# DMA transposes, and a first batch pipelined by head pairs, in a fused attention and MLP kernel

## The chip, the cores and the metric

The kernel runs on one core of one Trainium2 chip. The metric is the device time of the whole program in microseconds (us), as the median over several executions; lower is better.

## The reference, cut to what matters

There are 8 batches, 12 heads, 448 positions and a head size of 64, so the model width is 768.

```python
q_n, k_n = rmsnorm(q, g_q), rmsnorm(k, g_k)        # over the 64 of a head, gains per channel
attn = softmax(q_n @ k_n.T / 8)                    # 448 x 448 for each head
x = concat_heads(attn @ v)                         # batch x 448 x 768
u = x + ((x.T @ U) @ V).T                          # mixing along the sequence, rank 32
out = u + relu(u @ w_ch1) @ w_ch2                  # 768 -> 3072 -> 768
```

## The kernel before

Positions lie on partitions (112 at a time). A "pair" `p` is two heads; a "tile" `t` is four heads, so two pairs; a batch has six pairs and three tiles. q and k are normalised in that layout and must then be turned so that the head channel lies on partitions. The MLP needs u turned in the same way. Both are done on TensorE:

```python
def transposes(p):                                  # eight 112x128 blocks through TensorE
    pt = ps_o.tile([P, 2, S], BF16, tag="o")
    for s in range(2):
        for j in range(NJ):
            nc.tensor.transpose(pt[:, s, j * SP:(j + 1) * SP], qkn[...], ident[:SP, :SP])
    nc.vector.tensor_scalar(qT, pt[:, 0], gg, None, OP.mult)     # both gains, on the way out of PSUM
    nc.vector.tensor_copy(kT, pt[:, 1])

def mix_u(b, dc):                                   # u turned: low-rank part + x times identity
    nc.tensor.matmul(pu, t4s[b][:, ds], V4, start=True, stop=False)
    for i, off in enumerate(OFFS[par]):
        nc.tensor.matmul(pu[:, lo:hi], xt[i][:, ds], ident[:, ...], start=False, stop=(i == 3))
    ...                                             # copies to uA, uB

# in mlp(b): the low-rank product again, for the residual in the output layout
nc.tensor.matmul(po, V4[:, off:off + P], t4s[b][:, hs], start=True, stop=False)
for hc in range(KH):
    nc.tensor.matmul(po, hT[:, hc, i * P:(i + 1) * P], w2b[:, hc, hs], start=False, ...)
```

The program first does the attention and the mixing of batch 0 (the "head"), and then, for each batch, weaves the attention of the next batch between the MLP products of this one. Every engine runs its own instructions in program order; the first hole below shows it (ACT stood still for 10.34 us before one instruction, while the exponential behind it had its scores ready).

```python
for _, piece in attention(0, head=True): piece()
for _, piece in mixing(0): piece()
for b in range(B):
    fill, total = mlp(b), volume(b % 2)
    weave(fill, total * 0.86, attention(b + 1))     # attention spread over 86% of the MLP
    weave(fill, total * 0.11, mixing(b + 1))
```

## Time and profile before

The time is 657.54 us (657.22 to 657.66, 3 executions). PE is TensorE, PEld the loading of its weights, DVE is VectorE, ACT is ScalarE, POOL is GpSimd, SP is the engine that issues most DMAs.

| | before |
|---|---|
| profiled span | 655.2 us |
| first MLP product (end of the head) | 67.3 us |
| PE busy from there to the end | 582 of 588 us |
| PE busy in the head from 20 to 60 us | 52% to 62% |

This is the table of stretches of the kernel before; it gives the busy us of each engine in each stretch, in the order PE, PEld, DVE, ACT, POOL, with the number of instructions, then the granted TensorE clock, the mean busy share of the DMA engines, and GB/s.

```profile
20.00:30.00 10.00, 6.01 (x56) 3.53 (x56) 7.59 (x13) 4.63 (x7) 6.73 (x5) 0.50 0.77 122
30.00:40.00 10.00, 6.22 (x69) 3.83 (x68) 6.06 (x18) 4.36 (x5) 1.66 (x1) 0.67 1.18 253
40.00:50.00 10.00, 5.16 (x56) 3.42 (x57) 5.60 (x14) 3.73 (x6) 10.00 (x9) 0.50 1.06 213
67.20:655.00 587.80, 582.33 (x4834) 332.05 (x4834) 303.60 (x682) 202.51 (x302) 89.60 (x57) 1.00 0.28 70
```

In the head PE is half idle and its clock is cut to 0.50 to 0.67. From the first MLP product on, PE is full at full clock. DMA is over-full (above 1) from 30 us on, because the weights come in; it stays so until about 90 us.

This is the chain of waits of the kernel before, inside one MLP: start, length, what. (The chain is followed back from the last instruction, at each step to what released it.)

```profile
236.42 1.08 PE ph L286 x6
237.50 0.39 PE pt L190 x8
237.89 1.95 PE ph L286 x12
```

```profile
281.13 0.19 PE pu L263
281.32 0.20 PE pu L266 x4
281.51 0.97 PE po L306 x6
```

The chain is nothing but PE here, one group behind the other, so its lengths are prices: eight transposes cost 0.39 to 0.40 us, one mixing group 0.39 us, six output products 0.97 us (0.162 each).

### The profile page before, as it was taken

The numbers are of one execution on the slowest core, as the hardware profiler recorded it, in microseconds if no ns is written. First come the engines' busy times: TensorE is split into PE (matmuls) and PEld (weight loads), VectorE is DVE, ScalarE is ACT, GpSimd is POOL, SyncE is SP. The second block draws the span as 40 slices with busy tenths as digits, with TensorE's granted clock in tenths as the row PEclk, the third lists the DMA queues.
The fourth block names the chain that finished last, engine by engine and source line by source line (L and its number), as shares of the span: only waits on it lengthen the run. The fifth ranks groups of instructions, "written<-read, shape, count | busy, mean of one in ns | idle before, by whom it ended". The sixth has DMA issues, their size and how long they took to land.

```text
span 655.2 us, 12039 instructions
## 1 busy us (share of the span) xinstructions
PE 623.4 (95%) x5198; PEld 355.5 (54%) x5198; DVE 346.3 (53%) x773; ACT 231.0 (35%) x341; POOL 120.8 (18%) x98
## 2 busy tenths in 40 slices
PE   6556999999999999999999999999999999999997
PEld 2334565654556555654456556654556656554464
DVE  4757766555544575565644666655544465252211
ACT  5443453244431444224522254315432164402100
POOL 2465132202202022202202022202020200000000
PEclk9566999999999999999999999999999999999999
DMA  7999983421305213503305033413314100010011
GB/s 171 171 234 225 226 184 89 110 72 38 86 25 133 70 41 85 133 26 85 86 25 131 27 86 86 109 49 85 78 32 105 54 2 2 25 49 1 0 50 48
DMA packets 47445, 54.59 MB, mean 83 GB/s; under 512 B 3744, under 2 KB 43808, under 8 KB 47392
## 3 DMA queue, kind: packets, MB, share of 16 engines
q1 hardware_dynamic: 39200, 44.39, 26.8%
q0 software_dynamic: 7872, 9.44, 8.4%
q8 instruction: 40, 0.66, 0.4%
q14 instruction: 13, 0.11, 0.1%
q10 hardware_dynamic: 320, 0.00, 0.0%
HBM read 52.25 MB, written 11.01 MB: 97 GB/s over the span
## 4 chain that ended last, share of the span: by engine, by line
PE 89%; DVE 3%; ACT 2%; DMA 1%; POOL 1%; issue 0%; POOLq 0%
PE po L306 34%; PE ph L286 33%; PE o L225 8%; PE sc L204 7%; PE pt L190 3%; PE pu L263 2%; PE pu L266 2%; ACT E_95 L209 1%; DMA qk<-in_q_dram 1%; PE po L304 1%; DVE rstd L165 1%; DVE qkn L179 1%; ACT hT L289 1%; PE pm L250 1%; POOL sq L160 1%
## 5 line engine op out<-in xcount | busy, mean ns | idle before, releaser
L306 PE MATMUL po<-w2b,hT 128*128 128x384 bf16 x1344 | 244.5, 326 | 0.0
L306 PEld LDWEIGHTS <-hT 128*128 128x128 bf16 x1344 | 124.5, 98 | 82.6 <-issue 10.3
L286 PEld LDWEIGHTS <-w1b 128*128 128x128 bf16 x1152 | 104.5, 98 | 98.8 <-issue 14.2
L160 POOL TENSOR_TENSOR sq<-qk 112x1024 f32<-112x1024 f32 x44 | 83.2, 1907 | 381.9 <-DVE rstd L165 188.8
L289 ACT ACTIVATE hT<-ph 128x384 bf16<-128x384 f32 (+1 forms) x96 | 52.1, 543 | 234.1 <-PE ph L286 234.1
L286 PE MATMUL ph<-uB,w1b 128*128 128x512 bf16 x576 | 133.0, 379 | 0.0
L209 ACT ACTIVATE E_96<-sc 112x896 bf16<-112x896 f32 x96 | 86.2, 911 | 80.4 <-PE sc L204 80.3
L209 ACT ACTIVATE E_95<-sc 112x896 bf16<-112x896 f32 x96 | 85.4, 912 | 60.2 <-PE sc L204 60.2
L286 PE MATMUL ph<-uA,w1b 128*128 128x384 bf16 x576 | 105.3, 326 | 0.1
L291 DVE TENSOR_SCALAR hT<-ph 128x384 bf16<-128x384 f32 (+1 forms) x96 | 59.8, 623 | 83.9 <-PE ph L286 83.5
L179 DVE TENSOR_TENSOR qkn<-qk,rstd 112x512 bf16<-112x512 f32 x96 | 66.6, 734 | 1.8 <-ACT rstd L171 1.4
L204 PE MATMUL sc<-qT,kT 64*112 64x448 bf16 x384 | 63.2, 394 | 2.9 <-ACT E_95 L209 1.2
L165 DVE TENSOR_REDUCE rstd<-sq 112x16 f32<-112x1024 f32 x48 | 56.3, 1210 | 10.1 <-ACT sq L158 6.6
L228 DVE RECIPROCAL rec<-o 128x4 f32<-128x4 f32 x96 | 17.3, 180 | 62.0 <-PE o L225 61.6
L194 DVE TENSOR_SCALAR qT<-pt,gg 128x448 bf16<-128x448 bf16 x48 | 21.5, 448 | 46.7 <-PE pt L190 46.6
L225 PEld LDWEIGHTS <-E_95 112*128 112x128 bf16 x768 | 32.1, 101 | 20.1 <-DVE xs_100 L232 8.6
L204 PEld LDWEIGHTS <-kT 64*112 64x112 bf16 x384 | 20.7, 130 | 37.7 <-issue 34.2
L225 PEld LDWEIGHTS <-E_96 112*128 112x128 bf16 x768 | 32.3, 102 | 12.2 <-DVE xs_100 L232 3.9
L190 PE MATMUL pt<-ident,qkn 112*128 112x112 bf16 x384 | 28.5, 218 | 5.9 <-DVE qkn L179 4.8
L190 PEld LDWEIGHTS <-qkn 112*128 112x128 bf16 x384 | 23.9, 100 | 16.3 <-DVE qkn L179 7.1
L272 DVE CAST uB<-pu 128x448 bf16<-128x448 f32 x24 | 14.5, 620 | 8.6 <-PE pu L266 8.6
L195 DVE COPY kT<-pt 128x448 bf16<-128x448 bf16 x48 | 18.3, 381 | 0.0
(102 smaller groups left out, 354.7 us busy)
## 6 DMA issues: line engine op xcount, KB each, us to landing
qk<-in_q_dram SPq DMA_DIRECT2D x24, 448.0 KB, 4.4
qk<-in_k_dram SPq DMA_DIRECT2D x24, 448.0 KB, 5.9
vt<-in_v_dram SPq DMA_DIRECT2D x24, 448.0 KB, 6.8
w1b<-in_moe_w_ch_dram POOLq DMA_DIRECT2D x6, 768.0 KB, 12.3
w2b<-in_moe_w_ch_dram POOLq DMA_DIRECT2D x6, 768.0 KB, 28.4
out_dram<-osb SPq DMA_DIRECT2D x8, 336.0 KB, 2.8
out_dram<-osb SPq DMA_DIRECT2D x8, 288.0 KB, 2.7
out_dram<-osb SPq DMA_DIRECT2D x8, 240.0 KB, 2.6
```

Source lines behind the costliest of these rows:

```text
L160: nc.gpsimd.tensor_tensor(sqs[t, s], qks[t][:, s], qks[t][:, s], OP.mult)
L165: nc.vector.tensor_reduce(rstds[t][:, s].rearrange("p h j -> p (h j)"), sqs.pop((t, s)).rearrange("p h (j d) -> p (h j) d", d=D), AX, OP.add)
L179: nc.vector.tensor_tensor(qkns[t][:, pr, s].rearrange("p j h d -> p h j d"), qk[:, s, hp].rearrange("p h (j d) -> p h j d", d=D), rstd[:, ...
L190: nc.tensor.transpose(pt[:, s, j * SP:(j + 1) * SP], qkn[:, p % 2, s, j].rearrange("p h d -> p (h d)"), ident[:SP, :SP])
L194: nc.vector.tensor_scalar(qT, pt[:, 0], gg, None, OP.mult)
L204: nc.tensor.matmul(sc[:, hh, 0:S], kT[pp, kc * SP:(kc + 1) * SP], qT[pp, :], start=True, stop=True)
L209: nc.scalar.activation(Es[p % NE][:, :, PAD + kc * S:PAD + (kc + 1) * S], scs.pop((p, kc))[:, :, 0:S], AF.Exp, scale=float(D) ** 0.5)
L225: nc.tensor.matmul(o[:, i, :], E[:, hh, c:c + P], va[:, hl, kc, :], start=(kc == 0), stop=(kc == NJ - 1))
L286: nc.tensor.matmul(ph, w1b[:, dc, hc * P:(hc + 1) * P], u[:, dc, :], start=(dc == 0), stop=(dc == KD - 1))
L289: nc.scalar.activation(hT[:, hc, 0:n], ph, AF.Relu)
L291: nc.vector.tensor_relu(hT[:, hc, 0:n], ph)
L306: nc.tensor.matmul(po, hT[:, hc, i * P:(i + 1) * P], w2b[:, hc, hs], start=False, stop=(hc == KH - 1))
```

## The change

The intent is to take work off the full TensorE, and to shorten the head:

- The transposes of q and k become one DMA transpose per pair, except for the first 8 pairs. The gains are then a separate VectorE step.
- The mixing adds the low-rank part to x in place, in the output layout; u is turned by DMA. The output stage no longer repeats the low-rank product.
- Batch 0 is a pipeline by head pairs: its mixing is done per pair on TensorE, the first load is split in halves, pair 6 (of batch 1) runs in the head too, and filler products are to hold the clock up.
- The squares of tile 2 move from POOL to ACT, and are computed in pair 0. The attention of the next batch is pressed into 77% of the MLP (86% before), so that 14% stay for the DMA transposes of u to land.

```diff
-    NE, NV, NWARM, NFILL = 2, 3, 30, 0
+    NE, NV, NWARM, NH = 2, 3, 16, 3
+    FA, FM, NPE = 0.77, 0.09, 8
@@ squares
-            if t < 2:
+            if t < 3:
                 nc.scalar.activation(...Square)
@@ transposes
+        if p < NPE:
+            ...                                   # on TensorE, as before
+        else:
+            nc.sync.dma_start_transpose(qkT.rearrange("d s (j p) -> d (s j) p", j=NJ), qkn)
+    def gains(p):
+        if p >= NPE:
+            nc.vector.tensor_scalar(qkTs[p][:, 0], qkTs[p][:, 0], gg, None, OP.mult)
@@ mixing
+    def mix_u(b, i):                              # for two halves of 384 columns
+            nc.tensor.matmul(pu, lhsT, t4s[b][:, hs], start=True, stop=True)
+            nc.vector.tensor_add(xt[rows, hs], pu[rows, :], xt[rows, hs])
+    def mix_uT(b, i):
+            nc.sync.dma_start_transpose(us[b][:, :, i * P:(i + 1) * P], ...)
@@ mlp
-                    nc.tensor.matmul(po, V4[:, off:off + P], t4s[b][:, hs], start=True, stop=False)
@@ attention, one pair (cut): scores, expo, transposes(p+1), ..., values(p-1, 0)
+            add(0, scale, t + 1, odd)
             add(1, scores, p, (2, 3))
             ...
             add(1, values, p - 1, 1)
             ...
+                add(0, gains, p + 1)              # last VectorE step before the next pair's scores
             ...
             add(0, load, t + 3)                   # every second pair
@@ head (cut)
+        load(0, 2); load(1); load_v(0); ...
+        squares(1); scale(0, 1)
+        load_mix()                                # 14 small DMAs of U, one of V
+        load(2); load_v(1); load_v(2)
+        cast_v(0); load_w1(0); load_w1(1)
+        for p in range(7):
+            scores(p, (0, 1)); expo(p, 0)
+            if p > 1: mix_a(0, p - 2)
+            transposes(p + 1)
+            ...                                   # heat(NH): three filler products, twice a pair
+            squares(t + 2, ss=(odd,))             # at p = 0 this is tile 2, on ACT
+            expo(p, 3)
+            ...
@@ schedule
+        head()
+        for i in range(6): load_w2(i)
+                rest = [mix_u(0, i) for i in range(4)] + attention(1, 1)
```

More of the change, by code (lines that the diff above doesn't have):

```diff
@@ L113, in load_mix @@
                     nc.sync.dma_start(Uf[r:r + p1 - p0, par, i, :], Ur[j, p0:p1, :])
-        for i in range(4):
-            nc.sync.dma_start(Vf[i * rank:(i + 1) * rank, :], moe_V)
+        nc.sync.dma_start(Vf, moe_V.rearrange("r s -> () r s").to_broadcast([4, rank, S]))
     def setup_mix():
@@ L135, with load @@
     NT, NP = B * 3, B * 6
-    qks, vts, sqs, rstds, qkns, qTs, scs, x3_of = {}, {}, {}, {}, {}, {}, {}, {}
-    def load(t):
-        b, h0 = t // 3, (t % 3) * HG
-        qk = loads.tile([SP, 2, HG, NJ * D], FP32, tag="qk")
-        nc.sync.dma_start(qk[:, 0], q[b, h0:h0 + HG].rearrange("h (p j) d -> p h (j d)", j=NJ))
-        nc.sync.dma_start(qk[:, 1], k[b, h0:h0 + HG].rearrange("h (p j) d -> p h (j d)", j=NJ))
-        qks[t] = qk
+    qks, vts, sqs, rstds, qkns, qkTs, scs, x3_of = {}, {}, {}, {}, {}, {}, {}, {}
+    def load(t, parts=1):
+        b, h0, n = t // 3, (t % 3) * HG, HG // parts
+        qks[t] = loads.tile([SP, 2, HG, NJ * D], FP32, tag="qk", name="qk")
+        for h in range(0, HG, n):
+            for s, src in enumerate((q, k)):
+                nc.sync.dma_start(qks[t][:, s, h:h + n],
+                                  src[b, h0 + h:h0 + h + n].rearrange("h (p j) d -> p h (j d)", j=NJ))
     def load_v(t):
@@ L152, in cast_v, with squares, reduce, rsqrt @@
         nc.gpsimd.tensor_copy(vas[t % NV][:, :, :, 0:D], vts.pop(t).rearrange("p h (j d) -> p h j d", d=D))
-    def squares(t):
-        for s in range(2):
-            sqs[t, s] = norm.tile([SP, HG, NJ * D], FP32, tag="sq", name="sq")
-            if t < 2:
-                nc.scalar.activation(sqs[t, s], qks[t][:, s], AF.Square)
-            else:
-                nc.gpsimd.tensor_tensor(sqs[t, s], qks[t][:, s], qks[t][:, s], OP.mult)
-    def reduce(t):
-        rstds[t] = norm.tile([SP, 2, HG, NJ], FP32, tag="rstd", name="rstd", bufs=3)
-        for s in range(2):
-            nc.vector.tensor_reduce(rstds[t][:, s].rearrange("p h j -> p (h j)"),
-                                    sqs.pop((t, s)).rearrange("p h (j d) -> p (h j) d", d=D), AX, OP.add)
-    def rsqrt(t):
-        rs = rstds[t].rearrange("p s h j -> p (s h j)")
+    ALL = slice(0, HG)
+    def squares(t, hs=ALL, ss=(0, 1)):
+        for s in ss:
+            if (t, s) not in sqs:
+                sqs[t, s] = norm.tile([SP, HG, NJ * D], FP32, tag="sq", name="sq")
+            if t < 3:
+                nc.scalar.activation(sqs[t, s][:, hs], qks[t][:, s, hs], AF.Square)
+            else:
+                nc.gpsimd.tensor_tensor(sqs[t, s][:, hs], qks[t][:, s, hs], qks[t][:, s, hs], OP.mult)
+    def reduce(t, hs=ALL, ss=(0, 1)):
+        if t not in rstds:
+            rstds[t] = norm.tile([SP, 2, HG, NJ], FP32, tag="rstd", name="rstd", bufs=3)
+        for s in ss:
+            nc.vector.tensor_reduce(rstds[t][:, s, hs].rearrange("p h j -> p (h j)"),
+                                    sqs[t, s][:, hs].rearrange("p h (j d) -> p (h j) d", d=D), AX, OP.add)
+    def rsqrt(t, hs=ALL):
+        rs = rstds[t][:, :, hs].rearrange("p s h j -> p s (h j)")
         nc.scalar.activation(rs, rs, AF.Ln, bias=eps)
@@ L185, in transposes @@
     def transposes(p):
-        qkn = qkns[p // 2]
-        pt = ps_o.tile([P, 2, S], BF16, tag="o")
-        for s in range(2):
-            for j in range(NJ):
-                nc.tensor.transpose(pt[:, s, j * SP:(j + 1) * SP],
-                                    qkn[:, p % 2, s, j].rearrange("p h d -> p (h d)"), ident[:SP, :SP])
-        qT = attn.tile([P, S], BF16, tag="qT")
-        kT = attn.tile([P, S], BF16, tag="kT")
-        nc.vector.tensor_scalar(qT, pt[:, 0], gg, None, OP.mult)
-        nc.vector.tensor_copy(kT, pt[:, 1])
-        qTs[p] = qT, kT
+        qkn = qkns[p // 2][:, p % 2].rearrange("p s j h d -> p (s j) (h d)")
+        qkT = attn.tile([P, 2, S], BF16, tag="qkT")
+        qkTs[p] = qkT
+        if p < NPE:
+            pt = ps_mm.tile([P, 2, S], BF16, tag="mm")
+            for i in range(2 * NJ):
+                nc.tensor.transpose(pt.rearrange("d s (j p) -> d (s j) p", j=NJ)[:, i, :], qkn[:, i, :], ident[:SP, :SP])
+            nc.vector.tensor_scalar(qkT[:, 0], pt[:, 0], gg, None, OP.mult)
+            nc.vector.tensor_copy(qkT[:, 1], pt[:, 1])
+        else:
[3 more added lines that the diff above has]
+            nc.vector.tensor_scalar(qkTs[p][:, 0], qkTs[p][:, 0], gg, None, OP.mult)
     def scores(p, kcs):
-        qT, kT = qTs[p]
+        qT, kT = qkTs[p][:, 0], qkTs[p][:, 1]
         for kc in kcs:
@@ L220, in values @@
         d0 = (2 * (p % 6) + hh) * D
-        o = ps_o.tile([P, 4, D + 1], FP32, tag="o")
+        if p < 6 and hh:
+            o = ps_mm.tile([P, 4, D + 1], FP32, tag="mm")
+        else:
+            o = ps_o.tile([P, 4, D + 1], FP32, tag="o")
         for i, off in enumerate(OFFS[par]):
@@ L253, in mix_t @@
         t4s[b] = t4b
-    def mix_u(b, dc):
-        par = b % 2
-        if dc == 0 and par == 0:
-            us["A"] = upool.tile([P, KD, 384], BF16, tag="uA", name="uA")
-            us["B"] = upool.tile([P, KD, 512], BF16, tag="uB", name="uB")
-        uA, uB, xt = us["A"], us["B"], x_tiles(b)
-        ds = slice(dc * P, (dc + 1) * P)
-        pu = ps_mm.tile([P, S], FP32, tag="mm")
-        nc.tensor.matmul(pu, t4s[b][:, ds], V4, start=True, stop=False)
-        for i, off in enumerate(OFFS[par]):
-            lo, hi = max(off, 0), min(off + P, S)
-            nc.tensor.matmul(pu[:, lo:hi], xt[i][:, ds], ident[:, lo - off:hi - off],
-                             start=False, stop=(i == 3))
-        if par == 0:
-            nc.vector.tensor_copy(uA[:, dc, :], pu[:, 0:384])
-            nc.vector.tensor_copy(uB[:, dc, 0:64], pu[:, 384:448])
-        else:
-            nc.vector.tensor_copy(uB[:, dc, 64:512], pu)
+    def mix_u(b, i):
+        par, off = b % 2, OFFS[b % 2][i]
+        lhsT = V4[:, off:off + P] if 0 <= off < 384 else Vsh[:, par, :]
+        rows = slice(0, P) if 0 <= off < 384 else slice(64 * par, 64 * par + 64)
+        xt = x_tiles(b)[i]
+        for half in range(2):
+            hs = slice(half * HALF, (half + 1) * HALF)
+            pu = ps_mm.tile([P, HALF], FP32, tag="mm")
+            nc.tensor.matmul(pu, lhsT, t4s[b][:, hs], start=True, stop=True)
+            nc.vector.tensor_add(xt[rows, hs], pu[rows, :], xt[rows, hs])
@@ new lines, in mix_uT, with mix_a @@
+    def mix_uT(b, i):
+        par, off = b % 2, OFFS[b % 2][i]
+        if i == 0:
+            us[b] = upool.tile([P, KD, 384 + 128 * par], BF16, tag=f"u{par}", name=f"u{par}")
+        if par or off < 384:
+            nc.sync.dma_start_transpose(us[b][:, :, i * P:(i + 1) * P],
+                                        x_tiles(b)[i].rearrange("t (c d) -> t c d", d=P))
+    def mix_a(b, dc):
+        xt, cs = x_tiles(b), slice(dc * P, (dc + 1) * P)
+        if dc == 0:
+            us[b] = upool.tile([P, KD, 384], BF16, tag="u0", name="u0")
+            t4s[b] = upool.tile([P, dm], BF16, tag="t4b", bufs=3, name="t4b")
+        pm = ps_mm.tile([P, P], FP32, tag="mm")
+        for i in range(4):
+            nc.tensor.matmul(pm[i * rank:(i + 1) * rank, :], Ub[:, b % 2, i, :], xt[i][:, cs], start=True, stop=True)
+        nc.vector.tensor_copy(t4s[b][:, cs], pm)
@@ L275, in store, with mix_b @@
+    def mix_b(b, dc):
+        xt, cs = x_tiles(b), slice(dc * P, (dc + 1) * P)
+        pu = ps_mm.tile([P, 384], FP32, tag="mm")
+        nc.tensor.matmul(pu, t4s[b][:, cs], V4[:, 0:384], start=True, stop=False)
+        for i in range(3):
+            nc.tensor.matmul(pu[:, i * P:(i + 1) * P], xt[i][:, cs], ident, start=False, stop=(i == 2))
+        nc.vector.tensor_copy(us[b][:, dc, :], pu)
     def store(b, c0, c1, osb, r0):
@@ L281, in mlp @@
         par = b % 2
-        u, n = (us["A"], 384) if par == 0 else (us["B"], 512)
+        u, n = us[b], (384, 512)[par]
         for hc in range(KH):
@@ L299, in mlp @@
                 po = ps_mm.tile([P, HALF], FP32, tag="mm")
-                if off < 0:
-                    nc.tensor.matmul(po, Vsh[:, 0, :], t4s[b - 1][:, hs], start=True, stop=False)
-                    nc.tensor.matmul(po, Vsh[:, 1, :], t4s[b][:, hs], start=False, stop=False)
-                else:
-                    nc.tensor.matmul(po, V4[:, off:off + P], t4s[b][:, hs], start=True, stop=False)
                 for hc in range(KH):
                     nc.tensor.matmul(po, hT[:, hc, i * P:(i + 1) * P], w2b[:, hc, hs],
-                                     start=False, stop=(hc == KH - 1))
+                                     start=(hc == 0), stop=(hc == KH - 1))
                     if hc % 6 == 5 and hc != KH - 1:
@@ L317, in mlp, with attention @@
                 yield HALF
-    def attention(b, head=False):
+    def attention(b, start=0):
         items = []
@@ L324, in add @@
             items.append((weight, lambda: fn(*args)))
-        for p in range(b * 6, b * 6 + 6):
+        for p in range(b * 6 + start, b * 6 + 6):
             t, odd = divmod(p, 2)
-            late = head and p == 0
             add(1, scores, p, (0, 1))
             add(0, expo, p, 0)
-            if head and p == 1:
-                add(0, scale, 1, 0)
             if p + 1 < NP:
                 add(1, transposes, p + 1)
-            if odd and t + 2 < NT:
-                add(0, reduce, t + 2)
-            if late:
-                add(0, reduce, 1)
             add(1, expo, p, 1)
+            if not odd and t + 1 < NT:
+                add(0, rsqrt, t + 1)
             if p % 6:
                 add(1, values, p - 1, 0)
-            if not odd:
-                if t + 1 < NT and not late:
-                    add(0, scale, t + 1, 0)
-                if t + 2 < NT:
-                    add(0, squares, t + 2)
+            if t + 1 < NT:
+                add(0, scale, t + 1, odd)
             add(1, scores, p, (2, 3))
             add(0, expo, p, 2)
-            if odd and t + 2 < NT:
-                add(0, rsqrt, t + 2)
             if p % 6:
                 add(1, values, p - 1, 1)
-            if t + 1 < NT and (p == 1 if head and t == 0 else not odd):
-                add(0, scale, t + 1, 1)
+            if t + 2 < NT:
+                add(0, squares, t + 2, ALL, (odd,))
+            if t + 1 < NT and odd:
                 add(0, cast_v, t + 1)
+            if p + 1 < NP:
+                add(0, gains, p + 1)
+            add(1, expo, p, 3)
+            if t + 2 < NT:
+                add(0, reduce, t + 2, ALL, (odd,))
             if odd and t + 3 < NT:
@@ L358, in attention @@
                 add(0, load_v, t + 3)
-            add(1, expo, p, 3)
-            if late:
-                add(0, rsqrt, 1)
-            if head and p == 2:
-                add(0, setup_mix)
-            if head and p in (0, 2, 3):
-                for i in range((0, 0, 2, 4)[p], (2, 0, 4, 6)[p]):
-                    add(0, load_w1, i)
         add(1, values, b * 6 + 5, 0)
@@ L369, in attention, with head @@
         return items
+    def head():
+        A, Bh = slice(0, 2), slice(2, 4)
+        load(0, 2)
+        load(1)
+        load_v(0)
+        setup()
+        heat(NWARM)
+        squares(0, A)
+        reduce(0, A)
+        squares(0, Bh)
+        rsqrt(0, A)
+        scale(0, 0)
+        nc.vector.tensor_mul(gg, gg, gk2)
+        transposes(0)
+        reduce(0, Bh)
+        rsqrt(0, Bh)
+        squares(1)
+        scale(0, 1)
+        load_mix()
+        load(2)
+        load_v(1)
+        load_v(2)
+        cast_v(0)
+        load_w1(0)
+        load_w1(1)
+        for p in range(7):
+            t, odd = divmod(p, 2)
+            scores(p, (0, 1))
+            expo(p, 0)
+            if p > 1:
+                mix_a(0, p - 2)
+            transposes(p + 1)
+            if p == 0:
+                reduce(1)
+            expo(p, 1)
+            if not odd:
+                rsqrt(t + 1)
+            if p:
+                values(p - 1, 0)
+            if p == 6:
+                values(5, 1)
+                mix_b(0, 4)
+                mix_a(0, 5)
+            elif p < 6:
+                heat(NH)
+            scores(p, (2, 3))
+            expo(p, 2)
+            if p == 6:
+                mix_b(0, 5)
+            elif p:
+                values(p - 1, 1)
+            if 1 < p < 6:
+                mix_b(0, p - 2)
+            scale(t + 1, odd)
+            if p == 1:
+                setup_mix()
+            squares(t + 2, ss=(odd,))
+            expo(p, 3)
+            reduce(t + 2, ss=(odd,))
+            if p < 6:
+                heat(NH)
+            if odd:
+                cast_v(t + 1)
+                load(t + 3)
+                load_v(t + 3)
+            if p in (1, 2):
+                load_w1(2 * p)
+                load_w1(2 * p + 1)
     def mixing(b):
-        return [(1, lambda: mix_t(b))] + [(1, lambda dc=dc: mix_u(b, dc)) for dc in range(KD)]
+        items = [(1, lambda: mix_t(b))]
+        for i in range(4):
+            items.append((1, lambda i=i: (mix_u(b, i), mix_uT(b, i))))
+        return items
     def weave(fill, total, items):
@@ L396 @@
     with tc.manual_schedule():
-        load(0)
-        load(1)
-        load_v(0)
-        load_v(1)
-        setup()
-        heat(NWARM)
-        squares(0)
-        reduce(0)
-        rsqrt(0)
-        scale(0, 0)
-        nc.vector.tensor_mul(gg, gg, gk2)
-        transposes(0)
-        squares(1)
-        scale(0, 1)
-        load(2)
-        load_v(2)
-        load_mix()
-        cast_v(0)
-        for _, piece in attention(0, head=True):
-            piece()
-        for _, piece in mixing(0):
-            piece()
+        head()
         for i in range(6):
@@ L423 @@
             if b + 1 < B:
-                weave(fill, total * 0.86, attention(b + 1))
-                weave(fill, total * 0.11, mixing(b + 1))
+                rest = [(1, lambda i=i: mix_u(0, i)) for i in range(4)] + attention(1, 1)
+                weave(fill, total * FA, attention(b + 1) if b else rest)
+                weave(fill, total * FM, mixing(b + 1))
             for _ in fill:
```

## The prediction

> **What bounds the kernel now.** TensorE, in two regimes. In the table of stretches, PE is busy 582 of the 588 us from 67.2 us (first MLP product) to the end, at full clock; the chain of waits is 89% PE. The first 67 us are a dependent chain: PE busy about 60%, granted clock 0.50 to 0.74 from 20 to 70 us, waits for q/k loads (8.7 us at 29.5 in the chain) and for squares on POOL, and a mixing stage (62.2 to 67.2) that nothing overlaps. PE work removed after 67 us counts in full; in the head only the chain counts.
>
> **What goes off PE after 67 us**, costed by the step from start to start in the timeline at full clock, not by latency (a 128x384 product lasts 326 ns, but they follow each other every 162 ns):
> - q/k transposes: eight take 0.51 us; 41 pairs: -20.9 us. (64 stay, for pairs 0 to 7.)
> - Low-rank product repeated in the output stage: 64 x 0.162 = -10.4 us.
> - Mixing to u: 42 groups of 0.39 us (16.4) become 64 products of 0.162 us (10.4): -6 us. Batch 0's second mixing is among the 64.
> - Scores of pair 6 move into the head: -1 us.
>
> Sum -38 us. DVE (53% busy) sheds PSUM copies and stays off the path.
>
> **What is added.** 40 q/k and 24 to 28 u transposes on SP's one queue, between loads and stores. The Trainium skill, "VectorE: DVE Perf Modes", section "The three transpose paths", gives 1309 ns for a 128x128 bf16 transpose by DMA, 390 ns on TensorE; this trace shows 218 ns latency and 64 ns step on TensorE, and no DMA transpose. As one instruction moves eight blocks, I estimate 3 to 6 us from issue to landing. A pair takes 8 to 10 us in the steady state, so q/k transposes should mostly be hidden; the gain multiplication on DVE, which waits for the landing, may hold DVE briefly. The u transposes have to land within the last 14% of the MLP, 6.5 to 8.6 us: tight. The first ones also meet saturated DMA engines (share above 1 until 90 us). I charge 6 us of PE stalls, perhaps 0 to 25.
>
> **Head.** The split first load brings the first scores from 13.2 to about 10 us. The mixing stage and the wait before it (about 10 us) get hidden in the pairs, but a seventh pair is added. DVE sets the pace, about 6 us a pair (sum of reduce, scale, copies, values, mixing). Squares of tile 2 move to ACT, in pair 0, while its load is queued behind 14 small U loads (9.9 us of issue): ACT should stall until about 20 us, which eats part of the gain. Fillers should raise the granted clock to near 1, but DVE and loads then bind. I expect the first MLP product at 57 us (50 to 63): -10 us. If w2 is issued late, behind POOL squares waiting for loads, a few us are lost.
>
> **Prediction.** 657.5 - 38 - 10 + 6, rounded down a little: 613 us, 8 in 10 between 596 and 634. Faster by over 2%: 0.89; within 2%: 0.07; slower: 0.04.
>
> **Right if** the PE step within the MLP is unchanged and two batches are about 11 us shorter than the 151 us of before; the head's granted clock is above 0.8; the first MLP product is at 50 to 63 us; PE waits for u or qkT transposes total under 10 us. **Wrong if** transposes land in over 8 us or issue slowly on SP: then PE waits at each batch boundary for u, DVE waits at the gains, and stores and loads queue behind; or if w2 or tile loads hold up batch 0.

## More of the kernel before

Where the text splits a run by stages, the times come from the profiled execution of that kernel, which is a single one.

## The result, and the profile after

The changed kernel takes 659.61 us (658.88 to 661.09, 4 executions), against 657.38 us for the kernel before in the same rounds. The ratio is 1.004, with a 95% interval from 1.0017 to 1.0062. (Ratios here are the mean time of one kernel's fast runs over that of the other's of the same rounds, so not quite the ratio of the medians.) No gain came of it: 46 us of the prediction are missing.

Cut by stages at the first MLP product of a batch, in the two profiled executions:

| stage | before, us | changed, us | predicted change | measured change |
|---|---|---|---|---|
| head | 67.3 | 74.1 | -10 | +6.8 |
| MLP of batch 0 | 67.8 | 80.2 | -4.8 | +12.4 |
| MLPs of batches 1 to 6 | 451.3 | 437.7 | -31.9 | -13.6 |
| MLP of batch 7 | 68.8 | 67.2 | -1.6 | -1.6 |
| span | 655.2 | 659.2 | -48 and +6 of waits | +4.0 |

The column of predictions splits the prediction's 38 us by where the instructions stood: for batches 1 to 6 it is 35 pairs x 0.51, 48 output products x 0.162, and 36 mixing groups x 0.39 less 48 x 0.162.

These are stretches of the changed kernel, with the columns of before:

```profile
20.00:30.00 10.00, 0.40 (x2) 0.13 (x2) 0.84 (x2) 0.32 (x1) 0.00 (x0) 0.66 1.18 242
100.00:110.00 10.00, 2.06 (x14) 1.16 (x13) 1.40 (x5) 1.30 (x2) 3.96 (x3) 0.76 1.11 213
74.10:659.00 584.90, 554.55 (x4291) 306.87 (x4288) 298.26 (x641) 200.84 (x300) 96.71 (x64) 0.99 0.43 95
```

Two holes stand out. From 20 to 30 us hardly any engine works (PE 0.40 us, DVE 0.84, ACT 0.32), and from 100 to 110 us PE works for 2 us of 10. In both the DMA engines are over-full. From the first MLP product on, PE is now idle for 30 us (584.90 - 554.55) where it was idle for 5.5.

This is the view of waits, PE alone, of the changed kernel from 74 to 154.3 us (batch 0's MLP), and then from 154.3 to 592 us (batches 1 to 6); for the kernel before, the same view is empty from 135 to 586 us.

```profile
PE sc L213 <- DVE qkT L205: 9.1, 3, 7.9
PE pu L276 <- DVE x_284 L277: 1.6, 1, 1.6
...
```

```profile
PE sc L213 <- DVE qkT L205: 5.6, 7, 1.8
PE po L334 <- DVE osb L338: 2.6, 9, 0.3
PE o L237 <- DVE xs_101 L244: 2.2, 2, 1.3
PE o L237 <- DVE xs_100 L244: 1.3, 1, 1.3
```

A line says who waited for whom, for how long in total, how often, and the longest. `qkT L205` is the new gain step: the scores wait for it in both stages, once for 7.9 us.

**The first hole.** This is the timeline of the changed kernel around it, cut: start, length, engine, what, and in brackets the idle time before and what ended it.

```profile
14.65 1.84 POOL L128 DMA_DIRECT2D w1b<-in_moe_w_ch_dram  x2
...
17.59 0.41 SPq L143 DMA_DIRECT2D qk<-in_q_dram  x1
...
30.66 1.06 ACT L162 ACTIVATE sq<-qk 112x1024 f32<-112x1024 f32 x1 [10.34 <-DMA qk<-in_q_dram]
...
32.58 0.62 PE L213 MATMUL sc<-qkT 64*112 64x448 bf16 x2 [11.81 <-ACT E_95 L218]
```

The load of tile 2 is issued at 17.59 us, behind the 14 small loads of U on SP, and after two pieces of w1 had started from POOL. It lands 13 us later. ACT has the squares of tile 2 in its order before the last exponential of pair 0, so ACT stops, then the scores of pair 1, then everything. The Trainium skill, "DMA: Bandwidth & Descriptors", section "Issuing engines are not separate DMA queues", says that DMAs from different engines run on the same 16 DMA engines and interleave; this trace agrees, with a busy share of 1.18 and 242 GB/s while the tile is late. In its packets from 22 to 27 us, w1 takes about 0.7 of the DMA engines' time, and SP's loads of 1 KB packets, tile 2 among them, 0.31 to 0.35.

**The second hole.** This is the chain of waits of the changed kernel in batch 0's MLP:

```profile
90.80 0.56 DVE hT L324
91.83 17.41 DMA qkT<-qkn
109.27 0.35 DVE qkT L205
109.75 1.00 PE sc L213 x4
```

A DMA transpose took 17.4 us from issue to landing. It was issued directly behind a tile load (three DMAs of 448 KB from 90.39 us) on the same queue, while w2, issued at 75.7 us, filled the DMA engines. The profile's page lists the issues of the whole kernel, with the median time to landing as its last number:

```profile
qkT<-qkn SPq DMA_TRANSPOSE x40, 3.3
```

The same list for 75 to 115 us alone:

```profile
qkT<-qkn SPq DMA_TRANSPOSE x3, 13.9
```

These three are all the DMA transposes of q and k in that stretch. The view of their tile in the changed kernel gives their shortest, median and longest time to landing, and below it stands the same for 154 to 301 us, where the weights are in:

```profile
DMA to landing us min/median/max: 6.4/13.9/17.4
DMA to landing us min/median/max: 2.9/3.1/6.9
```

Neither the tile load nor w2 makes the 17.4 us alone. The 13.9 us belong to the transpose issued at 76.99 us, beside w2, when the tile load before it had just landed (at 77.1 us). The 6.9 us belong to a transpose right behind a tile load, with w2 long in. In the packets of the trace, those of the 17.4 us transpose move only from 106 us on, as w2 and the tile load end. SP itself was held as well: issuing that transpose took it 11.7 us, where the quickest took 1.2. So a transpose is fast when the DMA engines are free, slower behind a tile load, and slowest behind one while the weights come in.

**The small waits later.** This is the timeline of the changed kernel in an even batch, cut:

```profile
269.25 3.75 POOL L164 TENSOR_TENSOR sq<-qk 112x1024 f32<-112x1024 f32 x2 [13.81 <-DMA qk<-in_q_dram]
...
271.84 3.14 DVE L184 TENSOR_TENSOR qkn<-qk,rstd 112x512 bf16<-112x512 f32 x2
...
275.49 0.17 DVE L240 RECIPROCAL rec<-o 128x4 f32<-128x4 f32 x1
...
276.33 0.34 DVE L205 TENSOR_SCALAR qkT<-qkT,gg 128x448 bf16<-128x448 bf16 x1
...
276.81 0.58 PE L213 MATMUL sc<-qkT 64*112 64x448 bf16 x4 [1.78 <-DVE qkT L205]
```

The gain step stands last in VectorE's order, behind the scale step, the evictions and the reciprocal. The scale step (a pair of instructions) took 3.14 us here, and 1.27 to 1.33 wherever POOL was idle or all but idle beside it; POOL was squaring at the same time. The Trainium skill, "SBUF — State Buffer", section "Who interferes with whom", says that a VectorE instruction with two SBUF inputs contends with a GpSimd instruction that reads SBUF. This trace fits it; no run isolates it.

### The profile page after: what moved, and what is told of

The parts are those of the page before. It is cut to its first block, busy times and chain, and to the rows that moved or that the text cites. A ratio compares the mean times of both kernels' runs of the same rounds, so it can differ in the third digit from the quotient of the medians.

```text
span 659.2 us, 11159 instructions
## 1 busy us (share of the span) xinstructions
PE 599.2 (91%) x4700; PEld 329.7 (50%) x4700; DVE 338.8 (51%) x737; ACT 233.9 (35%) x347; POOL 117.2 (18%) x96
## 4 chain that ended last, share of the span: by engine, by line
PE 77%; DMA 9%; DVE 8%; ACT 2%; issue 1%; SPq 1%; POOL 1%; DVEq 0%; POOLq 0%
PE po L334 32%; PE ph L319 30%; PE o L237 7%; PE sc L213 6%; DMA qk<-in_q_dram 4%; DVE qkn L184 3%; DMA qkT<-qkn 3%; DVE osb L338 1%; DMA vt<-in_v_dram 1%; DVE rstd L170 1%; PE pu L276 1%; ACT hT L322 1%; ACT E_96 L218 1%; DVE hT L324 1%; ACT E_95 L218 1%
## 5 line engine op out<-in xcount | busy, mean ns | idle before, releaser
L334 PE MATMUL po<-w2b,hT 128*128 128x384 bf16 x1344 | 235.2, 326 | 2.9 <-DVE osb L338 2.9
L319 PEld LDWEIGHTS <-w1b 128*128 128x128 bf16 x1152 | 106.7, 98 | 106.7 <-issue 17.6
L164 POOL TENSOR_TENSOR sq<-qk 112x1024 f32<-112x1024 f32 x42 | 79.0, 1896 | 370.9 <-DMA qk<-in_q_dram 354.0
L218 ACT ACTIVATE E_96<-sc 112x896 bf16<-112x896 f32 x96 | 85.6, 914 | 71.1 <-PE sc L213 71.1
L213 PE MATMUL sc<-qkT 64*112 64x448 bf16 x384 | 61.9, 384 | 29.9 <-DVE qkT L205 14.7
L184 DVE TENSOR_TENSOR qkn<-qk,rstd 112x512 bf16<-112x512 f32 x96 | 70.5, 774 | 17.9 <-ACT rstd L176 17.3
L170 DVE TENSOR_REDUCE rstd<-sq 112x16 f32<-112x1024 f32 (+1 forms) x50 | 58.2, 1167 | 23.8 <-ACT sq L162 15.5
L213 PEld LDWEIGHTS <-qkT 64*112 64x112 bf16 x384 | 21.5, 128 | 69.1 <-issue 56.8
L237 PEld LDWEIGHTS <-E_95 112*128 112x128 bf16 x768 | 31.7, 101 | 16.1 <-issue 10.6
L237 PEld LDWEIGHTS <-E_96 112*128 112x128 bf16 x768 | 30.1, 98 | 11.8 <-DVE xs_100 L244 3.0
L319 PE MATMUL ph<-u_5020,w1b 128*128 128x512 bf16 x144 | 33.3, 379 | 0.0
L319 PE MATMUL ph<-u_1608,w1b 128*128 128x512 bf16 x144 | 33.3, 379 | 0.0
L319 PE MATMUL ph<-u_3314,w1b 128*128 128x512 bf16 x144 | 33.3, 379 | 0.0
L319 PE MATMUL ph<-u_6686,w1b 128*128 128x512 bf16 x144 | 31.2, 379 | 0.0
L319 PE MATMUL ph<-u_367,w1b 128*128 128x384 bf16 x144 | 28.1, 343 | 1.0 <-ACT hT L322 0.5
L319 PE MATMUL ph<-u_5889,w1b 128*128 128x384 bf16 x144 | 25.8, 326 | 0.0
L319 PE MATMUL ph<-u_2477,w1b 128*128 128x384 bf16 x144 | 25.6, 326 | 0.0
```

The source lines that it names most:

```text
L164: nc.gpsimd.tensor_tensor(sqs[t, s][:, hs], qks[t][:, s, hs], qks[t][:, s, hs], OP.mult)
L170: nc.vector.tensor_reduce(rstds[t][:, s, hs].rearrange("p h j -> p (h j)"), sqs[t, s][:, hs].rearrange("p h (j d) -> p (h j) d", d=D), AX, ...
L184: nc.vector.tensor_tensor(qkns[t][:, pr, s].rearrange("p j h d -> p h j d"), qk[:, s, hp].rearrange("p h (j d) -> p h j d", d=D), rstd[:, ...
L213: nc.tensor.matmul(sc[:, hh, 0:S], kT[pp, kc * SP:(kc + 1) * SP], qT[pp, :], start=True, stop=True)
L218: nc.scalar.activation(Es[p % NE][:, :, PAD + kc * S:PAD + (kc + 1) * S], scs.pop((p, kc))[:, :, 0:S], AF.Exp, scale=float(D) ** 0.5)
L237: nc.tensor.matmul(o[:, i, :], E[:, hh, c:c + P], va[:, hl, kc, :], start=(kc == 0), stop=(kc == NJ - 1))
```

## The experiments

Twelve runs were made, each correct unless said otherwise. Four went on one chip together, then four, then three, then one; the kernel before measured 656.76, 657.12, 657.30 and 657.57 us beside them. The table lists the stages of each profiled execution.

| run | median, us | ratio to before (95%) | head | batch 0 | batches 1 to 6 | batch 7 |
|---|---|---|---|---|---|---|
| before | 657.4 | 1 | 67.3 | 67.8 | 451.3 | 68.8 |
| changed | 659.61 | 1.004 | 74.1 | 80.2 | 437.7 | 67.2 |
| npe48 | 660.09 | 1.005 (1.0034 to 1.0066) | 73.2 | 70.7 | 446.4 | 67.2 |
| npe12 | 650.64 | 0.990 (0.989 to 0.992) | 74.7 | 69.8 | 437.5 | 67.5 |
| nogain | 653.16 | 0.994 (0.992 to 0.996) | 74.2 | 77.5 | 432.3 | 67.2 |
| load2 | 640.85 | 0.977 (0.975 to 0.979) | 59.9 | 74.1 | 435.4 | 67.3 |
| nh0 | 661.21 | 1.006 (1.003 to 1.008) | 74.6 | 79.7 | 438.3 | 67.2 |
| gearly | 635.61 | 0.967 (0.965 to 0.970) | 59.5 | 73.5 | 432.3 | 67.3 |
| gearly_fa82 | 637.13 | 0.968 (0.965 to 0.971) | 61.7 | 75.4 | 430.8 | 67.2 |
| gearly_npe12 | 632.50 | 0.962 (0.959 to 0.965) | 57.2 | 71.7 | 432.3 | 67.5 |
| gearly_npe48 | 647.63 | 0.984 (0.981 to 0.987) | 57.5 | 71.1 | 446.2 | 67.2 |
| latemix | 631.92 | 0.962 (0.960 to 0.963) | 61.9 | 68.5 | 432.3 | 67.5 |
| w2early | 630.96 | 0.960 (0.959 to 0.961) | 62.2 | 68.2 | 432.3 | 67.5 |
| noadd | 627.21 | 0.952 (0.950 to 0.955) | 60.3 | 69.8 | 429.7 | 67.5 |

The stage of batches 1 to 6 repeats to a tenth of a us between kernels that are alike in it. The head does not: among the kernels with the early load it ends between 57 and 62 us, for a reason that no run shows, so medians of those kernels that differ by under 3 us are not told apart by it.

### npe48: all q/k transposes on TensorE

```diff
-    FA, FM, NPE = 0.77, 0.09, 8
+    FA, FM, NPE = 0.77, 0.09, 48
```

> The changed kernel with every q/k transpose on TensorE (40 pairs more, u still by DMA). Theory A (the DMA transposes of q and k cost about 17 us of waits: 9 us in batch 0's MLP, where one of them queues behind a tile load and w2, some 3 us of reduced clock after it, and 6 us of scores waiting for the gains in the later batches): TensorE work rises by 40 x 0.51 = 20 us, the waits go, so 660 to 667 us. Rival B (DMA transposes are what eats the whole missing 46 us): 640 us or less. The first MLP product stays at 72 to 76 us in both.

It took 660.09 us, as theory A said; rival B (DMA transposes cost the whole 46 us) falls. The stages show why the total is that of the changed kernel: batches 1 to 6 get 8.7 us longer (446.4 against 437.7), batch 0 gets 9.5 us shorter (70.7 against 80.2). The DMA transposes did save TensorE time; the late transpose in batch 0 gave it all back.

### npe12: only pairs 8 to 11 back on TensorE

```diff
-    FA, FM, NPE = 0.77, 0.09, 8
+    FA, FM, NPE = 0.77, 0.09, 12
```

> Only the transposes of pairs 8 to 11 (those issued while w2 loads) go back to TensorE. Theory A: +2 us of TensorE work, the 8 us wait near 101 to 109 us and the low clock after it go, so about 650 us (646 to 653). Rival B2 (the loads of w2 saturate the DMA engines and something else, such as the squares of the next tile, holds batch 0's MLP as long): 656 us or more, with another wait of 5 us or more between 75 and 125 us.

It took 650.64 us, and batch 0 went from 80.2 to 69.8 us. Nothing else took the place of the wait, so rival B2 falls.

### nogain: without the gain step (wrong results on purpose)

```diff
     def gains(p):
-        if p >= NPE:
-            nc.vector.tensor_scalar(qkTs[p][:, 0], qkTs[p][:, 0], gg, None, OP.mult)
+        pass
```

> The gain multiplication after the DMA transpose is left out (results are wrong on purpose: pairs 8 to 47 lack the gain), so scores wait for the landing of the transpose itself. Theory C (in the steady state the transposes land in time, about 3 us after issue, and the scores wait because the gain stands late in VectorE's order, behind scale, evictions and reciprocals): the waits of scores in the steady state, 5.6 us in all, go to under 1 us and two batches take about 144 us in place of 147; total 651 to 655; the 8 us wait in batch 0 stays, now on the DMA itself. Rival D (the landing of the transposes sets the pace): waits only change their name, 658 us or more.

It took 653.16 us; batches 1 to 6 got 5.4 us shorter, all in the even ones (batches 2 and 4 went from 68.1 to 65.4 us each). The waits of PE from 154.3 to 592 us in this run:

```profile
PE o L236 <- DVE xs L243: 2.9, 3, 1.0
PE po L333 <- DVE osb L337: 2.6, 9, 0.3
PE ph L318 <- issue: 0.5, 3, 0.2
```

No wait for the landing of a transpose took the place of the wait for the gains: theory C holds, rival D falls. In batch 0 the 7.7 us wait stays, on the DMA itself.

### load2: tile 2 loaded early, into a third buffer

```diff
-        qks[t] = loads.tile([SP, 2, HG, NJ * D], FP32, tag="qk", name="qk")
+        qks[t] = loads.tile([SP, 2, HG, NJ * D], FP32, tag="qk", name="qk", bufs=3)
         load_v(0)
+        load(2)
         setup()
 ...
         load_mix()
-        load(2)
         load_v(1)
```

(The t4b buffers go from 3 to 1 to make room.)

> A third q/k buffer, and the load of tile 2 is issued right behind the first loads, ahead of the small U loads and of w1 (the t4b buffers go from 3 to 1 to make room; they are not in use longer than one batch). Theory E (the head lost 10 us to ScalarE waiting, in its program order, for tile 2, whose load was queued behind the U loads and shared the DMA engines with w1): that wait at 20 to 30 us falls to under 2 us, the first MLP product comes at about 65 us in place of 74, total about 650 us. Rival F (the head is bound by bytes: the same bytes must come in, so the wait only moves to tiles 3 and 4): first MLP product at 71 us or later, total 656 us or more.

It took 640.85 us, 19 us less than the changed kernel and 9 less than theory E said. The same stretches as above, in this run:

```profile
20.00:30.00 10.00, 8.15 (x89) 4.75 (x91) 4.38 (x13) 6.07 (x8) 0.00 (x0) 0.83 1.22 218
100.00:110.00 10.00, 9.92 (x88) 5.54 (x85) 6.34 (x15) 5.24 (x9) 2.88 (x2) 1.00 0.20 39
```

The DMA engines are as full from 20 to 30 us, but PE works 8.15 us instead of 0.40: rival F falls, it was not the bytes but when tile 2 came. The edit does two things at once, an earlier place and a third buffer. In its old place tile 2 was not held up for want of a buffer: SP issued U and V one behind the other until 17.47 us, and tile 2 at 17.59. But tile 3 followed at 23.5 us in place of 39.7, and there its wait for a buffer (13.6 us in the view of waits of SP) went too; no run separates that part. The first MLP product comes at 59.9 us. As w2 is now issued at 57.4 us in place of 75.7, the second hole shrinks as well: the slowest transpose in batch 0 landed in 12.6 us, and the scores waited 2.3 us for the gains in place of 9.1.

### nh0: without the filler products in the pairs

```diff
-    NE, NV, NWARM, NH = 2, 3, 16, 3
+    NE, NV, NWARM, NH = 2, 3, 16, 0
```

> The changed kernel without the filler products inside the head's pairs (the 16 warm-up products stay). Theory G (the head is a chain over loads, ScalarE and VectorE, so the fillers neither help nor hurt much although the granted clock falls): 656 to 663 us, granted clock between 30 and 70 us lower than the 0.66 to 1.00 of before this edit. Rival H (the fillers buy time through the clock): 666 us or more. Rival I (the fillers stand in the way of scores and values): 654 us or less.

It took 661.21 us against 659.61, and the head ended at 74.6 us against 74.1. The granted clock from 50 to 74 us was 0.52 against 0.79 with fillers. So the fillers do hold the clock up, and here that buys about 2 us, no more than the scatter: a head that waits for loads and VectorE, as theory G had it, has little use for the clock.

### gearly: load2, and the gain step earlier in VectorE's order

```diff
             if t + 1 < NT:
                 add(0, scale, t + 1, odd)
+            if p + 1 < NP:
+                add(0, gains, p + 1)
             add(1, scores, p, (2, 3))
 ...
-            if p + 1 < NP:
-                add(0, gains, p + 1)
```

> The kernel of run load2, and the gain multiplication moved up in VectorE's order, to right behind the scale step of the same pair, ahead of the evictions of the second value product. Theory C (VectorE's order holds the scores): scores wait for the gains under 1 us after 150 us, even batches shorten from about 67 to about 65.5 us as in run nogain; total 634 to 638 us against 640.9. Rival D (the transpose has not landed so early): VectorE now waits for the DMA itself, 640 us or more.

It took 635.61 us, within the 634 to 638 of theory C. Batches 1 to 6 take 432.3 us, as in nogain, with correct results.

### gearly_fa82: attention over 82% of the MLP

```diff
-    FA, FM, NPE = 0.77, 0.09, 8
+    FA, FM, NPE = 0.82, 0.09, 8
```

> As gearly, with the attention of the next batch spread over 82% of the MLP in place of 77%. Theory J (attention pressed into 77% makes scores wait for exponentials, some 0.85 us each time, and the u transposes land 3 to 4 us before they are needed, so 2 to 3 us of the tail can be given back): 2 to 5 us less than gearly. Rival K (the tail is needed): first MLP products of a batch wait for u, by 1 to 3 us a batch, and the time is that of gearly or more.

It took 637.13 us: no gain in total, so theory J missed its numbers. The waits of PE from 216 to 281 us, an even batch and the first product of the odd one behind it:

```profile
PE ph L319 <- DMA u<-x: 0.9, 1, 0.9
PE ph L319 <- DVE hT L324: 0.6, 1, 0.6
PE po L334 <- DVE osb L338: 0.3, 1, 0.3
```

The first products of the odd batches now wait about 0.9 us for u (four waits, 3.7 us in the whole run), nearly what rival K said: there the tail is needed. The even batches don't wait. That fits the runs with 77%, where, as far as the traces show the landings, the last transpose of u lands 0.8 to 1.3 us before the first product of batches 1, 3 and 5, and about 4 to 5 us before that of an even batch, so theory J's 3 to 4 us held for the even ones only. Batches 1 to 6 are still 1.5 us shorter than in gearly, although 2.7 us of waits for u lie inside. That the total shows nothing of it is due to the head (2.2 us longer in the profiled execution, inside its scatter) and to batch 0 (1.9 us longer). In batch 0 VectorE reached the moved gain step before its transpose had landed, stood still there for 3.5 us, and PE then waited 4.3 us for an eviction behind it.

### gearly_npe12: gearly, and pairs 8 to 11 on TensorE

```diff
-    FA, FM, NPE = 0.77, 0.09, 8
+    FA, FM, NPE = 0.77, 0.09, 12
```

> As gearly, with pairs 8 to 11 transposed on TensorE. In the changed kernel this was worth 9 us. With the early load w2 is issued at 57 us in place of 76, and the wait of scores in batch 0 is only 2.3 us. If the gains of load2 and of npe12 have one cause in common, w2 landing late, then this run is within 3 us of gearly; if they are independent, it is 6 us or more below gearly.

It took 632.50 us, 3.1 us under gearly, against 9 us in the changed kernel. That is at the edge of the 3 us that the expectation named, and within the scatter; the stage is clearer. Batch 0 gains 1.8 us by it (73.5 to 71.7), where it gained 10.4 in the changed kernel. The gains of load2 and npe12 have most of their cause in common, w2 coming late.

### gearly_npe48: what the DMA transposes are worth in the mended kernel

```diff
-    FA, FM, NPE = 0.77, 0.09, 12
+    FA, FM, NPE = 0.77, 0.09, 48
```

> Run gearly_npe12 with all q/k transposes on TensorE: what the DMA transposes of pairs 12 to 47 are worth once the head, batch 0 and the gains no longer hide it. In the chain of the kernel before, eight transposes cost 0.40 us of TensorE, not the 0.51 of the prediction; 36 pairs x 0.40 = 14 us. Theory L (the gain was there but hidden): 645 to 648 us, against 632.5. Rival M (transposes by DMA save little in themselves, as the pair of runs after/npe48 with 659.6 and 660.1 us would say): 638 us or less.

It took 647.63 us, 15.1 us more than gearly_npe12; batches 1 to 6 take 446.2 against 432.3 us. That is 13.9 us for 35 pairs, or 0.40 us a pair, the price in the chain. Theory L holds, rival M falls. (The executions of this kernel scatter from 643.27 to 649.42 us, and the profiled one is the second fastest, so the 13.9 us of the stages carry this more than the 15.1 of the medians.)

### latemix: batch 0's second mixing moved to the middle of the next attention

```diff
-                rest = [(1, lambda i=i: mix_u(0, i)) for i in range(4)] + attention(1, 1)
+                late = attention(1, 1) if b == 0 else []
+                rest = late[:30] + [(1, lambda i=i: mix_u(0, i)) for i in range(4)] + late[30:]
```

> Run gearly_npe12 with the second mixing of batch 0 (the four in-place additions to x) moved from the start of batch 0's MLP to the middle of the next attention. Theory N (at the start VectorE is held by scale and reduce, 2 to 3 us each beside POOL, and TensorE waits 2.4 us for a mixing bank and then runs at reduced clock): batch 0 goes from 71.7 to 67 to 69 us, total 628 to 631. Rival O (the mixing only takes its wait along): within 1 us of gearly_npe12.

It took 631.92 us. (Of the expectation's 2 to 3 us each, the trace of gearly_npe12 has 2.98 for the scale step and 1.21 for the reduce.) Batch 0's MLP took 68.5 us in place of 71.7, but the head of the profiled run was 4.7 us longer, and the medians differ by 0.6 us. The total shows no gain; whether the shorter batch 0 is the edit's or only that of a later start is left open.

### w2early: latemix, and w2 issued before pair 6

```diff
         for p in range(7):
             ...
+            if p == 6:
+                for i in range(6):
+                    load_w2(i)
 ...
         head()
-        for i in range(6):
-            load_w2(i)
```

> As latemix, with the six w2 loads issued before pair 6 of the head instead of after it, ahead of POOL's squares of tile 5. If the time of w2's landing still costs batch 0 something, 1 to 3 us less than latemix; if the DMA engines are simply full until 90 us (share above 1.1), the tile loads land later instead, and it is equal to latemix or slower by 1 to 3 us, with a wait for tile 5 in the head.

It took 630.96 us, 1 us under latemix, inside the scatter. Nothing is settled by it, except that w2's place no longer matters much.

### noadd: gearly_npe12 without the in-place additions (wrong results on purpose)

```diff
             nc.tensor.matmul(pu, lhsT, t4s[b][:, hs], start=True, stop=True)
-            nc.vector.tensor_add(xt[rows, hs], pu[rows, :], xt[rows, hs])
```

> Run gearly_npe12 without the in-place additions of the mixing (wrong results on purpose: u is then plain x, but every product, transpose and store stays). Of the 14 us that the prediction took for the new mixing and the dropped output product in batches 1 to 6, the changed kernel with TensorE transposes shows 5. Theory P (the eight additions of 0.5 us a batch hold mixing banks, VectorE and the u transposes, so output products wait): each batch shortens by 1 us or more, total 624 us or less. Rival Q (the missing part is the attention pressed into 77% of the MLP, where scores wait for exponentials, which the additions do not touch): each batch shortens by under 0.5 us, total 629 us or more; batch 0 may lose its 2.4 us wait in both.

It took 627.21 us. Batches 1 to 6 shortened by 2.6 us, so 0.43 us each: under the limit of rival Q and far from theory P. The total lies between the two and scatters by 5 us (623.90 to 629.15), so it decides nothing.

## Why the prediction was right or wrong, point by point

Four steps of the prediction failed, and one price was off. In the head, "ACT should stall until about 20 us": it stalled until 30.7. In the waits, "I charge 6 us of PE stalls": PE waited 14.7 us for the gain step alone, 9.1 of them in batch 0. In the path, "DVE [...] stays off the path": that is how 5.6 of these waits came about. And in "PE work removed after 67 us counts in full": in batches 1 to 6, 13.6 us of 31.9 counted.

- **What bounds the kernel: right, but work removed counts in full only where nothing waits.** So it was in batch 7, which lost 1.6 us, its 10 output products at 0.162. It was not so in batches 1 to 6.
- **q/k transposes, -20.9 us: right in kind, mis-sized.** The prediction took 0.51 us for eight, or 64 ns from one transpose to the next. The trace of the kernel before has no such step. These are two rows of its timeline, at full clock:

```profile
96.37 0.56 PE L190 MATMUL pt<-ident,qkn 112*128 112x112 bf16 x8
96.77 2.12 PE L286 MATMUL ph<-uA,w1b 128*128 128x384 bf16 x12
```

From the start of the eight to the start of what follows it is 0.40 us, about 50 ns each, as in the chain of waits (0.39 to 0.40); npe12 against npe48 in the mended kernel measures 0.40 as well. Where the 64 ns came from the record doesn't show. For the 35 pairs of batches 1 to 6 that is 13.9 us, not 17.9.

- **Mixing and output products, 14.0 us in batches 1 to 6: gained, and for the most part lost again to waits.** The kernel before and npe48 both transpose q and k on TensorE; between them batches 1 to 6 differ by 4.9 us, so 9.1 are missing. The traces place them, if each PE instruction is counted from its start to the start of the next, so that a wait goes to the instruction before it. In batches 1 to 6 of gearly_npe48, against the kernel before, the value products took 4.0 us more (41.15 against 37.14), the scores 2.2 more (42.27 against 40.04) and the low-rank products of the mixing 0.8 more; mixing to u and the output products together fell by 12.0 us in place of 14.0. The first three, 7.0 us, are the price of pressing the attention into 77%: in gearly_fa82 all three are back within 0.2 us of the kernel before. (That kernel pays with other waits, for u and for evictions, so that only 1.5 us came of it.) The last 2.0 go with the additions: without them (noadd) the mixing products and the waits behind them take 8.1 us in place of 10.7, near the 7.8 of 48 products at 0.162.
- **"DVE stays off the path": wrong.** It is busy for half of the time, but it runs in order, and the gain step stood last before the scores that need it. That cost 5.4 us in batches 1 to 6 (nogain, gearly). The prediction saw the step ("may hold DVE briefly") but sought the cause in the landing.
- **Landing of a transpose, 3 to 6 us: right in the steady state** (median 3.3, and up to 6.9 behind a tile load), **wrong where it mattered**: 17.4 us while w2 came in. The prediction named this meeting and charged 6 us for all waits; batch 0 alone lost 9.5 us to it (80.2 against 70.7 in npe48). Its own warning, "transposes land in over 8 us or issue slowly on SP", came true on both counts there.
- **Head, first MLP product at 57 us: wrong by 17 us.** This is the step that failed first. The prediction saw that ACT would wait for tile 2, and put the end of that at 20 us from the U loads alone. It left out that two pieces of w1, issued 3 us earlier from another engine, share the DMA engines: the wait ended at 30.7 us. (No run moved w1 alone; load2 put tile 2 ahead of U and w1 both.) With the load moved (load2) the first product comes at 59.9 us, and at 57.2 to 62.2 in the kernels built on it, so the design of the head was worth about what was predicted, and the order of its loads was not. It pushed w2 back by 18 us too, into the DMA transposes of batch 0: the second hole.
- **"Transposes of u have to land in the last 14%: tight": right.** They cost no waits at 77%, and about 0.9 us in each odd batch at 82%.
- **"Fillers raise the clock, but DVE and loads bind": right** (nh0), though the clock was 0.66 to 0.83 in most of the head (1.00 in the first 10 us and from 40 to 50 us) and not near 1.

For batches 1 to 6 the sum closes: 31.9 predicted, less 4.0 for the transposes' price, 5.4 for the gain step, and 9.1 for mixing and output, gives 13.4 us; 13.6 were measured. As the 9.1 is itself the difference between two of these kernels, this shows only that the parts add up. That the totals before and after come out almost equal is chance: gains and losses happened to be of one size.

The mended kernels beat both: gearly_npe12, latemix and w2early take 631 to 632.5 us, 3.8% to 4.0% under the kernel before.

## What to carry to other kernels

Price work on a full engine from its start to the start of what follows, in a stretch at full clock, and check the price against the chain of waits. Before moving work to DMA, list what else is on the DMA engines at that moment, whichever engine issued it, and issue the load that an in-order engine will meet first before the bulk loads that can wait. A step that waits for a DMA needs a place in its engine's order well ahead of its consumer, even if that engine is half idle; but placed before the landing, it holds up all that stands behind it, as in batch 0 of gearly_fa82.

## What the Trainium skill lacked or had wrong

- "VectorE: DVE Perf Modes", section "The three transpose paths": it gives 390 ns (TensorE) and 1309 ns (DMA) for one 128x128 bf16 transpose. The section lacks the prices in a pipeline: eight 112x128 blocks cost 0.40 us of a full TensorE, 50 ns each; one DMA instruction with the same eight blocks lands in 3.3 us (median of the 35 whose landing the trace shows), far less than eight times 1309 ns.
- "DMA: Bandwidth & Descriptors", section "Rules for kernel authors": it says that a transpose next to ordinary DMAs needs nothing. That concerns the data, and the results here were correct; for the time the rule lacks a warning. Behind a tile load and beside w2 a transpose landed after 17.4 us in place of 3.3.
- The same page, section "Issuing engines are not separate DMA queues": agrees, with the load of tile 2 taking 13 us beside w1 at a DMA share of 1.18. It lacks the consequence for an in-order engine, 10.3 us of a stopped ACT.
- "TensorE: Matmul & The Clock Gate", section "Part 1: The HAM clock gate": it describes a cold and a warm clock set by recent activity, and the runs agree as to the direction: with filler products the granted clock from 50 to 74 us was 0.79, without them 0.52. It lacks the caution that a higher clock need not save time: here it bought about 2 us, no more than the scatter.
